# Two-branch layer on one core: all query tiles normalized inside the feed-forward, and the attention output of the last two heads moved into spare rows by DMA

## The chip, the cores and the metric

The kernel runs on one core of one Trainium2 chip. A core has a matrix engine (TensorE; PE in the profile, with its weight loads as PEld), a vector engine (VectorE; DVE), a scalar engine (ScalarE; ACT), a general engine (GpSimd; POOL) and a queue engine (SyncE; SP) that issues most of the transfers. Each engine takes its own instructions in order and waits for the others by semaphores. The metric is the time of the program on the device in microseconds (us); less is better.

## The reference

`x` has S = 2048 rows and D = 640 columns. Both branches read the layer norm of `x`; the result is `x + s * g`:

```python
xn = _layernorm(x, axis=-1)
# branch A: linear attention, H = 32 heads of Dh = 20
q, k, v = split(xn @ wqkv)
phi_q = concat([softmax(q @ w_phi), softmax(-(q @ w_phi))])     # 40 features a head; phi_k alike
kv = einsum("bhsf,bhsd->bhfd", phi_k, v);  z = einsum("bhsf->bhf", phi_k)
num = einsum("bhqf,bhfd->bhqd", phi_q, kv)
den = einsum("bhqf,bhf->bhq", phi_q, z)[..., None] + 1e-6
s = (num / den) @ wo
# branch B: feed-forward with F = 1536
g = silu(gelu(xn @ w1 + b1) @ w2 + b2)
return x + s * g
```

## The kernel before, in words

Precision: float32 operands are split into a high and a low part (hi, lo), and a product is three matmuls (hi with hi, and the two mixed ones), summed in PSUM. So most products are counted in threes (PASSES).

**Early stage** (to about 256 us): layer norm, projections to K, V and Q, the exponentials of the features, the state kv and z. The exponentials of the queries, not yet normalized, go to `e_dram`, sixteen tiles of 128 rows.

**Feed-forward** (256 to about 570 us): 12 units (halves of the rows times 6 groups of F columns; `units`), each about 25.8 us of TensorE: 54 "up" matmuls (L616), the activations (ScalarE L621 and its high copy L623, the low part on VectorE L627), then 60 "down" matmuls (L645) in two halves, `down(..., 0)` and `down(..., 1)`. The order on each engine is as the code is written out (manual schedule); nothing reorders it.

Into the units the **query normalization** is placed, tile by tile (`q_norm`): the tile is loaded from `e_dram` (L685), GpSimd multiplies it by z (L691), VectorE makes two reductions (L340) and some small operations, GpSimd scales the tile (L345), and SP stores it to `phi_dram` (L708). The table `QN` says which unit carries which tiles: units 1 to 5 one each, 7 to 9 two each, 10 one, 6 and 11 none. Tiles 4 to 7 are left to the last stage (`late_q`).

Weights are loaded raw (L144), split by ScalarE (L136, L400), GpSimd or VectorE (L138, L401). After unit 5 the half of the rows changes; the gate results of the first half of the units (`y0` to `y4`, called `held`) go through Silu in unit 6 and are stored to `g_dram` in unit 7 (L858). Buffers of 128 x 1280 or 128 x 1024 floats (`slab`) are shared in turn by eq, ez, hs, y and phi tiles: who gets a slab waits for its last user, the y store among them.

**Last stage** (from about 556 us): four chunks of 512 rows, in the order (2, 3, 0, 1). For each chunk `num_groups` transposes the normalized tiles (L735, copy L738), multiplies them with a block-diagonal form of kv (`bdk`, L746, for 30 heads in five groups j = 0 to 4; `bdl`, L753, for the last two heads, j = 5), and splits the outputs into `oT` tiles (hi on ScalarE L749, lo on VectorE L750). An `oT` tile holds six heads as 2 x 64 columns, of which 60 each are used. The last two heads have a tile of their own, `oTl`, with three copies of their 40 rows (120 rows: hi, hi and lo), selected by `lowsel` and `midsel`. Then `finish` makes the output blocks of 128 columns, five a chunk: 15 matmuls `oT` by `wo` and one `oTl` by `wol` (L804), which does the three passes at once; VectorE multiplies by the gate (L809), GpSimd adds x (L810; VectorE for the last blocks) and SP stores (L814). Gates of chunks 2 and 3 are loaded from `g_dram` (L788); those of chunks 0 and 1 come straight from the feed-forward through Silu on ScalarE (L796). x is loaded two blocks ahead (L784). The transposes and products of the next chunk are made between the blocks of the one before; those of the first chunk stand inside `down(..., 1)` of the last unit.

Transfers on SP are issued in the order of the code. SP's and ScalarE's transfers share eight semaphores in turn, so each one waits for the eighth before it.

Of the kernel before, what the change touches and what calls it, by code (L numbers as in the profile page):

```python
# [45 lines left out]
def hedgehog_gated_mlp_kernel(ctx: ExitStack, tc: tile.TileContext, x, xt_in, wqk, bd, wv, wo, w1, b1, w2, b2, out_t):  # L46
# [62 lines left out]
    for h in range(3):  # L109
# [4 lines left out]
    lowsel = const.tile([P, 1], F32, name="lowsel")  # L114
    nc.gpsimd.memset(lowsel[:], -1.0)
    nc.gpsimd.affine_select(out=lowsel[:], in_=lowsel[:], pattern=[[0, 1]],
                            compare_op=OP.is_ge, fill=0.0, base=-80, channel_multiplier=1)
    midsel = const.tile([P, 1], F32, name="midsel")
    nc.gpsimd.memset(midsel[:], -1.0)
    nc.gpsimd.affine_select(out=midsel[:], in_=midsel[:], pattern=[[0, 1]],  # L120
                            compare_op=OP.is_ge, fill=0.0, base=-40, channel_multiplier=1)
    nc.gpsimd.affine_select(out=midsel[:], in_=midsel[:], pattern=[[0, 1]],
                            compare_op=OP.is_ge, fill=0.0, base=79, channel_multiplier=-1)
    const.tile([P, 8], F32, name="align")
    bdk = const.tile([P, 10, 64], F32, name="bdk")
    bdl = const.tile([P, 120], F32, name="bdl")
# [436 lines left out]
    def kv_rest():  # L563
        kv_acc(NT - 1, phis.pop(NT - 1), vs.pop(NT - 1))
        kvr = const.tile([P, 360], F32, name="kvr")
        nc.gpsimd.memset(kvr[64:96, 320:360], 0.0)
        nc.gpsimd.memset(kvr[96:, 240:360], 0.0)
        for p, a, b in ((P, 0, 240), (96, 240, 320), (64, 320, 360)):
            nc.scalar.activation(kvr[:p, a:b], kvp[0][:p, a:b], AF.Copy)
        return kvr  # L570


    def kv_state(kvr):
        nc.gpsimd.memset(bdk[:, :, 60:], 0.0)
# [4 lines left out]
        nc.vector.tensor_tensor(bdk[:120, :, :60].rearrange("p f (h d) -> p f h d", d=20),  # L579
                                s3[:, :, None, :20].to_broadcast([120, 10, 3, 20]),  # L580
                                mask[:120, None, :, None].to_broadcast([120, 10, 3, 20]), op=OP.mult)
        for r in range(3):
            nc.vector.tensor_tensor(bdl[:80, 40 * r:40 * r + 40].rearrange("p (h d) -> p h d", d=20),
                                    ps[:80, None, 320:340].to_broadcast([80, 2, 20]),
                                    mask[:80, :2, None].to_broadcast([80, 2, 20]), op=OP.mult)
# [95 lines left out]

    def q_load(t):
        e = slab(F32, "eq")
        ef = e[:].rearrange("p a b -> p (a b)")
        nc.sync.dma_start(ef, e_dram[t])  # L685
        return ef

    def q_norm(t, ef):
        ez = slab(F32, "ez")
        zv = ez[:].rearrange("p a b -> p (a b)")  # L690
        nc.gpsimd.tensor_tensor(zv, ef, zf, op=OP.mult)  # L691
# [12 lines left out]
        nc.vector.tensor_tensor(r3, r3, den[:, :, None].to_broadcast([P, 32, 2]), op=OP.mult)  # L704
        yield
        scale_heads(ef, rc)
        yield
        nc.sync.dma_start(phi_dram[t], ef)  # L708

    def load_wol():  # L710
        raw = row([P, D], F32, "raw")
        for r in range(3):
            nc.sync.dma_start(raw[40 * r:40 * r + 40, :], wo[640:680, :])
        wol_h = row([P, D], F32R, "wolh")
        wol = row([P, D], F32R, "wol")
        nc.vector.tensor_copy(wol_h[:120, :], raw[:120, :])
        nc.vector.scalar_tensor_tensor(wol[:120, :], wol_h[:120, :].bitcast(F32), midsel[:120, :], raw[:120, :],
                                       op0=OP.mult, op1=OP.add)
        return wol


    def load_phi(c):
        tl = [slab(F32R, "phi", (P, 2 * D)) for _ in range(TPC)]
        for i in range(TPC):
            nc.sync.dma_start(tl[i][:].bitcast(F32), phi_dram[TPC * c + i])
        return tl
# [14 lines left out]
    def num_m(j, oT, p, n, ph):  # L741
# [9 lines left out]
        else:  # L751
            for a, b in ((0, 64), (64, 120)):
                nc.tensor.matmul(po[a:b, :256], bdl[:n, a:b], ph[:n, :256], start=True, stop=True)  # L753
            o2 = oT[1]
            nc.scalar.activation(o2[:120, 0, sl], po[:120, :256], AF.Copy)
            nc.vector.scalar_tensor_tensor(o2[:120, 1, sl], o2[:120, 0, sl].bitcast(F32), lowsel[:120, :],
                                           po[:120, :256], op0=OP.mult, op1=OP.add)

    def num_groups(phi, oT, size=4):
        steps = [(j, p) for p in range(2) for j in range(6)]  # L760
        before = []
        for k in range(0, 12, size):
            now = [(j, p, *num_t(phi, p, j)) for j, p in steps[k:k + size]]
            for j, p, n, ph in before:
                num_m(j, oT, p, n, ph)
            before = now
            yield
        for j, p, n, ph in before:
            num_m(j, oT, p, n, ph)
        yield  # L770
# [6 lines left out]
    ORDER = (2, 3, 0, 1)  # L777

    def load_res(i):
        if i < NCH * KC:  # L780
            c, d = divmod(i, KC)
            c = ORDER[c]
# [7 lines left out]
    def gate(i):  # L790
        if i < NCH * KC:
            c, d = divmod(i, KC)
            c = ORDER[c]
            if c < 2:
                y = ys[d][:, c, :]
                nc.scalar.activation(y, y, AF.Silu, bias=b2t[:, d:d + 1])  # L796
                gates[c, d] = y

    def finish(c, d, oT, last):
        ps = bankB()  # L800
        steps = [(wo_s[j][:, b, d * P:(d + 1) * P], oT[0][j][:, a, :]) for j in range(5) for a, b in PASSES]
        steps.append((wol[:120, d * P:(d + 1) * P], oT[1][:120, 1, :]))
        for n, (w, o) in enumerate(steps):
            nc.tensor.matmul(ps[:], w, o, start=n == 0, stop=n == 15)  # L804
        xr, gt = xres.pop((c, d)), gates.pop((c, d))
        for o in range(2):
            sl = slice(o * W2, (o + 1) * W2)
# [3 lines left out]
            if last:  # L811
                nc.sync.dma_start(out_t[d * P:(d + 1) * P, c * CW + o * W2:c * CW + (o + 1) * W2], xr[:, sl])
        if not last:
            nc.sync.dma_start(out_t[d * P:(d + 1) * P, c * CW:(c + 1) * CW], xr[:])  # L814
# [3 lines left out]
    QN = {1: (8,), 2: (9,), 3: (10,), 4: (11,), 5: (12,), 7: (13, 14), 8: (15, 0), 9: (1, 2), 10: (3,)}  # L818
    units = NH * NG

    def w2_raw(g):
        return [load_raw(w2[f * P:(f + 1) * P, :]) for f in range(g * GF, (g + 1) * GF)]

# [9 lines left out]
    for unit in range(units):  # L833
# [14 lines left out]
        else:  # L848
            wo_r = [load_raw(wo[j * P:(j + 1) * P, :]) for j in range(5)]
            phi = load_phi(ORDER[0])  # L850
# [55 lines left out]
        if not more:  # L906
# [4 lines left out]
            wo_s = [split_w(r[:], "wo", "pool", late) for j, r in enumerate(wo_r)]  # L911
# [4 lines left out]
        dn = down(g, w2g, hs, 0)  # L916
# [6 lines left out]
        next(dn)  # L923
        next(w1f, None)
# [12 lines left out]
        if not more:  # L937
            break
# [14 lines left out]
    wol = load_wol()  # L953
    oT = new_oT(late)
    qe[4] = q_load(4)
    load_res(0)
    load_res(1)
    for _ in down(g, w2g, hs, 1, num_groups(phi, oT, 3)):
        pass
# [3 lines left out]
    def late_q():  # L963
        qn = q_norm(4, qe.pop(4))
        next(qn)
        for t in range(4, 8):
            if t < 7:
                qe[t + 1] = q_load(t + 1)
            next(qn)
            yield  # L970
            next(qn)
            yield
            next(qn)
            next(qn)
            yield
            next(qn, None)
            if t < 7:
                qn = q_norm(t + 1, qe.pop(t + 1))
                next(qn)
            yield  # L980

    lq = late_q()
    for ci, c in enumerate(ORDER):
        nxt = iter(())
# [3 lines left out]
        for d in range(KC):  # L988
            load_res(ci * KC + d + 2)
            finish(c, d, oT, ci == NCH - 1 and d >= 3)  # L990
            next(lq, None)
            gate(ci * KC + d + 2)
            if ci == 0 and d % 2 == 0:
                next(lq, None)
            next(nxt, None)
            if ci + 2 < NCH and d == (0 if ci == 0 else 3):
                phin = load_phi(ORDER[ci + 2])
            next(lq, None)
        if ci + 1 < NCH:
            oT = oTn  # L1000
# [3 lines left out]
def _layout(A_x, A_wqkv, A_w_phi, A_wo, B_w1, B_b1, B_w2, B_b2):  # L1004
# [5 lines left out]
    wo = np.zeros((680, D), a["wo"].dtype)  # L1010
    for k in range(10):
        wo[64 * k:64 * k + 60] = a["wo"][60 * k:60 * k + 60]
    wo[640:] = a["wo"][600:]
# [37 lines left out]
```

## Time and profile before

| | |
|---|---|
| median of 3 runs | 686.83 us (685.87 to 687.21) |
| profiled execution | 688.63 us |
| its span in the trace | 686.9 us (1.7 us of the execution lie outside) |
| granted TensorE clock | 0.999 |
| HBM read and written | 79.85 and 45.10 MB, 182 GB/s over the span |

The span is cut into 40 slices in the page; a digit is the busy share in tenths:

```profile
PE   8899999999999999999999999999999999999997
DVE  4788566886876456677978774676977655774232
POOL 1355244859577355866968853636456640783221
```

A slice is 17.2 us. TensorE's line has nines from the third slice to the last but one: a high digit says that the engine has instructions nearly all the time, and only the chain of waits says whether the end hangs on them. VectorE and GpSimd vary by stage, and where both are near nine (around slice 25 and 31) the units carry two query tiles. Rows of other views are shown below where they are used. A row of the groups reads: line, engine, operation, tiles, shapes, count, then total busy time and mean of one. Where a matmul of the program shows as two records, the count of records is said.

### The profile page before, as it was taken

What the parts mean: (1) busy time and instruction counts of PE and PEld (TensorE: products, weight loads), DVE (VectorE), ACT (ScalarE), POOL (GpSimd) and SP (SyncE); (2) the same over time, 40 slices, a digit from 0 to 9 for tenths busy, and PEclk for the clock granted to TensorE, in tenths of its full rate; (3) what the DMA queues carried; (4) which work ended last, traced back from release to release, by engine and by line L of the source; (5) the groups of instructions that cost most, each with busy time, mean ns of one, the idle gap of its engine ahead of it and who ended that gap; (6) DMA issues with size and microseconds to landing.
All of it is one profiled execution on the core that took longest, in us unless ns stands there. A gap on an engine that the chain in (4) does not pass through costs nothing.

```text
span 686.9 us, 11941 instructions
## 1 busy us (share of the span) xinstructions
PE 676.7 (99%) x4713; PEld 590.6 (86%) x4713; DVE 455.5 (66%) x730; ACT 251.3 (37%) x398; POOL 375.6 (55%) x336
## 2 busy tenths in 40 slices
PE   8899999999999999999999999999999999999997
PEld 8899999999999998888887888888888887777875
DVE  4788566886876456677978774676977655774232
ACT  3332313323332237244353347633233354425430
POOL 1355244859577355866968853636456640783221
PEclk9999999999999999999999999999999999999999
DMA  9820052734261153329687697376364491886623
GB/s 339 305 88 2 3 150 81 242 79 149 51 216 59 80 171 134 115 70 329 211 301 260 210 421 319 90 266 240 140 206 153 145 396 49 314 295 210 231 93 107
DMA packets 73966, 125.73 MB, mean 183 GB/s; under 512 B 5694, under 2 KB 42558, under 8 KB 73014
## 3 DMA queue, kind: packets, MB, share of 16 engines
q1 hardware_dynamic: 71606, 114.48, 48.9%
q10 hardware_dynamic: 2304, 10.49, 4.2%
q8 instruction: 37, 0.61, 0.4%
q14 instruction: 19, 0.16, 0.1%
HBM read 79.85 MB, written 45.10 MB: 182 GB/s over the span
## 4 chain that ended last, share of the span: by engine, by line
PE 90%; DVE 5%; ACT 1%; issue 1%; DMA 1%; POOL 1%; SPq 0%; DVEq 0%; POOLq 0%; ACTq 0%
PE pA L306 30%; PE pB L645 22%; PE pB L616 18%; PE pB L804 11%; PE pB L746 3%; PE pB L735 2%; PE kv L377 2%; PE pA L163 2%; DVE y L654 2%; DVE xhi L670 1%; DMA xt<-in_x_dram 1%; PE pA L292 1%; PE pB L753 1%; DVE rc L340 0%; PE pB L590 0%
## 5 line engine op out<-in xcount | busy, mean ns | idle before, releaser
L645 PE MATMUL pB<-hs,w2s 128*128 128x512 f32 x720 | 167.1, 390 | 0.0
L645 PEld LDWEIGHTS pB<-hs,w2s 128*128 128x128 f32 x720 | 134.7, 188 | 29.2 <-PE pB L746 0.8
L616 PE MATMUL pB<-xp,w1s 128*128 128x512 f32 x324 | 81.4, 390 | 1.0 <-DVE pB L888 1.0
L616 PE MATMUL pB<-xd,w1s 128*128 128x512 f32 x324 | 79.3, 389 | 0.0
L332 ACT ACTIVATE e<-e 128x1280 f32<-128x1280 f32 x32 | 40.7, 1272 | 91.5 <-POOL e L327 91.0
L804 PE MATMUL pB<-oT,wo 128*128 128x512 f32 x300 | 72.9, 394 | 0.0
L616 PEld LDWEIGHTS pB<-xp,w1s 128*128 128x128 f32 x324 | 60.7, 188 | 13.9 <-DVE pB L888 1.4
L654 DVE TENSOR_TENSOR y<-pB,y 128x512 f32<-128x512 f32 x100 | 63.9, 680 | 12.3 <-PE pB L645 12.1
L616 PEld LDWEIGHTS pB<-xd,w1s 128*128 128x128 f32 x324 | 60.8, 188 | 12.6
L804 PEld LDWEIGHTS pB<-oT,wo 128*128 128x128 f32 x300 | 55.4, 188 | 14.8 <-ACT ph L738 1.2
L345 POOL TENSOR_TENSOR e<-e,rc 128x1280 f32<-128x1280 f32 x16 | 39.0, 2440 | 48.5 <-DVE rc L365 48.2
L345 POOL TENSOR_TENSOR eq<-eq,rc 128x1280 f32<-128x1280 f32 x16 | 38.0, 2372 | 50.0 <-DVE rc L704 50.0
L327 POOL TENSOR_TENSOR e<-nr,e 128x640 f32<-128x640 f32 x32 | 45.4, 1421 | 33.5 <-DVE nr L326 30.7
L306 PE MATMUL pA<-wv,xp 128*128 128x320 f32 x384 | 61.0, 312 | 0.8 <-DVE nr L326 0.4
L621 ACT ACTIVATE pB<-pB,b1t 128x512 f32<-128x512 f32 x48 | 31.8, 662 | 77.3 <-DVE pB L888 28.4
L306 PE MATMUL pA<-wk,xp 128*128 128x320 f32 x384 | 59.9, 311 | 0.0
L306 PE MATMUL pA<-wq,xp 128*128 128x320 f32 x384 | 59.0, 309 | 0.0
L306 PEld LDWEIGHTS pA<-wv,xp 128*128 128x128 f32 x384 | 56.9, 188 | 1.7 <-issue 0.7
L306 PEld LDWEIGHTS pA<-wq,xp 128*128 128x128 f32 x384 | 56.9, 188 | 0.1
L306 PEld LDWEIGHTS pA<-wk,xp 128*128 128x128 f32 x384 | 56.8, 188 | 0.1
L691 POOL TENSOR_TENSOR ez<-eq,zrep 128x1280 f32<-128x1280 f32 x16 | 47.3, 2953 | 1.1 <-PE pB L753 1.1
L401 POOL TENSOR_TENSOR w1s<-raw,w1s 128x640 fp32r<-128x640 f32 (+1 forms) x18 | 25.7, 1429 | 36.8 <-ACT w1s L400 29.6
(139 smaller groups left out, 1046.0 us busy)
## 6 DMA issues: line engine op xcount, KB each, us to landing
raw<-in_w_dram SPq DMA_DIRECT2D x42, 320.0 KB, 4.4
e_dram<-e ACTq DMA_DIRECT2D x16, 640.0 KB, 3.3
eq<-e_dram SPq DMA_DIRECT2D x16, 640.0 KB, 6.9
phi_dram<-eq SPq DMA_DIRECT2D x16, 640.0 KB, 3.4
phi<-phi_dram SPq DMA_DIRECT2D x16, 640.0 KB, 9.5
xt<-in_x_dram SPq DMA_DIRECT2D x16, 320.0 KB, 4.8
xres<-in_xt_dram SPq DMA_DIRECT2D x20, 256.0 KB, 4.5
out_dram<-xres SPq DMA_DIRECT2D x18, 256.0 KB, 3.0
```

The costliest lines, as they stand in the source:

```text
L306: nc.tensor.matmul(ps[:, hf, :HALF], stat_x(q, o, k, a), ws[k][:, b, hf * HALF:(hf + 1) * HALF], start=n == 0, stop=n == 3 * KC - 1)
L327: nc.gpsimd.tensor_tensor(e5[:, :, :, 1, :], nr[:, :, :, None].to_broadcast([P, 2, 16, DH]), e5[:, :, :, 0, :], op=OP.subtract)
L332: nc.scalar.activation(ef, ef, AF.Exp)
L345: nc.gpsimd.tensor_tensor(e3, e3, rc[:, :, None].to_broadcast([P, 64, DH]), op=OP.mult)
L401: nc.gpsimd.tensor_tensor(sl[:, 1, :n], src, sl[:, 0, :n].bitcast(F32), op=OP.subtract)
L616: nc.tensor.matmul(bank[ch][:], tl[:, a, off + wo_:off + wo_ + P], mov(blk, b), start=new and n == 0, stop=n == len(mms) - 1, skip_group_c ...
L621: nc.scalar.activation(ps, ps, AF.Gelu_apprx_tanh, bias=b1t[:, f:f + 1])
L645: nc.tensor.matmul(ps[:], ws[i][:, b, d * P:(d + 1) * P], hs[o][i][:, a, :], start=i == n == 0, stop=(i, n) == (GF - 1, 2), skip_group_che ...
L654: nc.vector.tensor_tensor(y, ps[:], y, op=OP.add)
L691: nc.gpsimd.tensor_tensor(zv, ef, zf, op=OP.mult)
L746: nc.tensor.matmul(po[64 * e:64 * e + 64, :256], bdk[:n, 2 * j + e, :], ph[:n, e * 256:(e + 1) * 256], start=True, stop=True)
L804: nc.tensor.matmul(ps[:], w, o, start=n == 0, stop=n == 15)
```

## The change

1. **Last two heads.** `wol`, `load_wol`, `lowsel` and `midsel` go. The columns of `bdk` are laid out anew: of each 16, 15 hold three heads' parts and every sixteenth is empty, and the rows of `wo` are laid out likewise, with the last two heads' 40 rows in the sixteenth places. `bdl` makes 40 columns with one matmul. The result, hi and lo, goes to `oTl` (40 rows), and `spread` moves 8 rows of it (32 KB) into rows 15, 31, 47, ... of each of the five `oT` tiles, by a DMA on ScalarE's queue, five a chunk. A block has 15 matmuls.
2. **Query tiles.** `QN` places all 16 in the units 1 to 11: one in each of 1 to 6, two in each of 7 to 11. `late_q` goes.
3. **Order.** Chunks run 0, 1, 2, 3, and groups in the order j = 5, 0, 1, 2, 3, 4. In the last unit, the splits of `wo` and the first chunk's products (sizes 2, 3, 3, 2, 2) start in the last call of `down(..., 0)`.
4. **Small moves.** In the last stage, output stores are issued one block later (`put`, `put_old`), and phi tiles are loaded one by one.

The core of the diff:

```diff
-    bdl = const.tile([P, 120], F32, name="bdl")
+    bdl = const.tile([P, 40], F32, name="bdl")
...
-    def load_wol():
...
-            for a, b in ((0, 64), (64, 120)):
-                nc.tensor.matmul(po[a:b, :256], bdl[:n, a:b], ph[:n, :256], start=True, stop=True)
+            nc.tensor.matmul(po[:40, :256], bdl[:n, :], ph[:n, :256], start=True, stop=True)
...
+    def spread(j, oT):
+        nc.scalar.dma_start(oT[0][j][15::16].bitcast(F32), oT[1][8 * j:8 * j + 8].bitcast(F32))
...
+    def num_groups(phi, oT, sizes=(4, 4, 4)):
+        steps = [(j, p) for j in (5, 0, 1, 2, 3, 4) for p in range(2)]
+        before, whole = [], []
+        def products(group):
+            for j, p, n, ph in group:
+                num_m(j, oT, p, n, ph)
+                if p and j < 5:
+                    whole.append(j)
+        def spreads():
+            while whole:
+                spread(whole.pop(0), oT)
+        for size in sizes:
+            now = [(j, p, *num_t(phi, p, j)) for j, p in steps[:size]]
+            del steps[:size]
+            spreads()
+            products(before)
+            before = now
+            yield
+        spreads()
+        products(before)
+        spreads()
         yield
...
-    ORDER = (2, 3, 0, 1)
+    ORDER = (0, 1, 2, 3)
...
-        steps.append((wol[:120, d * P:(d + 1) * P], oT[1][:120, 1, :]))
         for n, (w, o) in enumerate(steps):
-            nc.tensor.matmul(ps[:], w, o, start=n == 0, stop=n == 15)
+            nc.tensor.matmul(ps[:], w, o, start=n == 0, stop=n == 14)
...
-    QN = {1: (8,), 2: (9,), 3: (10,), 4: (11,), 5: (12,), 7: (13, 14), 8: (15, 0), 9: (1, 2), 10: (3,)}
+    QN = {1: (0,), 2: (1,), 3: (2,), 4: (3,), 5: (4,), 6: (5,), 7: (6, 7), 8: (8, 9), 9: (10, 11), 10: (12, 13), 11: (14, 15)}
...
+        dn = down(g, w2g, hs, 0, None if more else delayed(groups, 4))
```

Three places show how the instructions stand. The first is SP's queue at units 6 and 7 (raw is a weight row, eq a query tile, phi_dram its normalized form, y a stored gate; "x2" is two in a row). Before:

```order
L660 DMA xp<-xp_dram 128x2048
L708 DMA phi_dram<-eq 128x1280
L144 DMA raw<-in_w_dram 128x640 x4
L685 DMA eq<-e_dram 128x1280 x2
L144 DMA raw<-in_w_dram 128x640 x2
L685 DMA eq<-e_dram 128x1280 x2
L858 DMA g_dram<-y_3244 128x1024
L858 DMA g_dram<-y_3250 128x1024
```

And of the change:

```order
L651 DMA xp<-xp_dram 128x2048
L679 DMA phi_dram<-eq 128x1280
L134 DMA raw<-in_w_dram 128x640 x4
L688 DMA eq<-e_dram 128x1280 x2
L679 DMA phi_dram<-eq 128x1280
L134 DMA raw<-in_w_dram 128x640 x2
L688 DMA eq<-e_dram 128x1280 x2
L879 DMA g_dram<-y_3237 128x1024
L879 DMA g_dram<-y_3243 128x1024
```

A second phi_dram store (tile 5, which unit 6 now normalizes) stands ahead of two raw loads, two eq loads and the y stores.

The second is ScalarE in unit 7: the activations (L621, now L612) and the high copies into hs (L623, now L614), with what each waits for; a DMAHW semaphore is that of a transfer, here of a g_dram store that frees the slab. Before:

```order
L623 ACTIVATE hs<-pB 128x512 [waits DMAHW6_49,Activation_49]
L621 ACTIVATE pB<-pB,b1t 128x512 [waits DVE_49]
L623 ACTIVATE hs<-pB 128x512 [waits DMAHW7_49,Activation_49]
L621 ACTIVATE pB<-pB,b1t 128x512 [waits DVE_49]
L623 ACTIVATE hs<-pB 128x512 [waits PE_49,Activation_49]
```

And of the change:

```order
L614 ACTIVATE hs<-pB 128x512 [waits PE_49,Activation_49,Pool_49]
L612 ACTIVATE pB<-pB,b1t 128x512 [waits DVE_49]
L614 ACTIVATE hs<-pB 128x512 [waits PE_49,Activation_49,Pool_49]
L612 ACTIVATE pB<-pB,b1t 128x512 [waits DVE_49]
L614 ACTIVATE hs<-pB 128x512 [waits DMAHW0_49,Activation_49]
```

The wait for the first y store has moved from the first high copy of the unit to the third.

The third is TensorE at the start of the last stage (ph is the copy of the transposed tile; a bdk or bdl matmul of the program shows as two records in the trace). Before:

```order
L746 MATMUL pB<-ph,bdk 64x256 x4
L753 MATMUL pB<-ph,bdl 64x256
L753 MATMUL pB<-ph,bdl 56x256
L645 MATMUL pB<-hs,w2s 128x512 x6
L804 MATMUL pB<-oT,wo 128x512 x15
L804 MATMUL pB<-oTl,wol 128x512
L735 MATMUL pB<-identr,phi 120x128 x16
```

And of the change:

```order
L739 MATMUL pB<-ph,bdk 64x256 x4
L636 MATMUL pB<-hs,w2s 128x512 x6
L808 MATMUL pB<-oT,wo 128x512 x15
L728 MATMUL pB<-identr,phi 80x128 x4
L728 MATMUL pB<-identr,phi 120x128 x8
L808 MATMUL pB<-oT,wo 128x512 x15
L728 MATMUL pB<-identr,phi 120x128 x16
```

The last products ahead of the first block are now those of the fifth group of bdk instead of bdl's, then six down matmuls, and the block has 15 matmuls, the last three of which read the fifth oT tile.

More of the change, by code (lines that the diff above doesn't have):

```diff
@@ L113, in hedgehog_gated_mlp_kernel @@
                                 compare_op=OP.is_ge, fill=0.0, base=40 * h + 39, channel_multiplier=-1)
[L114 to L124, printed above, removed]
+    const.tile([P, 24], F32, name="align")
     bdk = const.tile([P, 10, 64], F32, name="bdk")
-    bdl = const.tile([P, 120], F32, name="bdl")
+    bdl = const.tile([P, 40], F32, name="bdl")
     def load_x(t):
@@ L564, in kv_rest @@
         kv_acc(NT - 1, phis.pop(NT - 1), vs.pop(NT - 1))
-        kvr = const.tile([P, 360], F32, name="kvr")
+        kvr = const.tile([P, 376], F32, name="kvr")
         nc.gpsimd.memset(kvr[64:96, 320:360], 0.0)
@@ L573, in kv_state @@
     def kv_state(kvr):
-        nc.gpsimd.memset(bdk[:, :, 60:], 0.0)
+        nc.gpsimd.memset(bdk[:, :, 15::16], 0.0)
         ps = bankB()
@@ L578, in kv_state @@
         s3 = ps[:120, :320].rearrange("p (f r) -> p f r", r=32)
[L579 to L585, printed above, removed]
+        for h in range(3):
+            nc.vector.tensor_scalar(
+                bdk[:120].rearrange("p f (q c) -> p f q c", c=16)[:, :, :, 5 * h:5 * h + 5],
+                s3[:, :, :20].rearrange("p f (q i) -> p f q i", i=5), mask[:120, h:h + 1], None, op0=OP.mult)
+        nc.vector.tensor_tensor(bdl[:80].rearrange("p (h d) -> p h d", d=20),
+                                ps[:80, None, 320:340].to_broadcast([80, 2, 20]),
+                                mask[:80, :2, None].to_broadcast([80, 2, 20]), op=OP.mult)
     def kv_norm(kvr):
@@ L679, in x_forms, with put, put_old @@
         nc.sync.dma_start(xd_dram[:, :, 1, at(p)], tt)
+    stores, late_store = [], [False]
+    def put(dst, src):
+        if late_store[0]:
+            stores.append((dst, src))
+        else:
+            nc.sync.dma_start(dst, src)
+    def put_old(n):
+        for _ in range(n):
+            nc.sync.dma_start(*stores.pop(0))
     def q_load(t):
@@ L707, in q_norm, with load_phi_tile @@
         yield
-        nc.sync.dma_start(phi_dram[t], ef)
-    def load_wol():
[L711 to L719, printed above, removed]
-    def load_phi(c):
[L723 to L726, printed above, removed]
+        put(phi_dram[t], ef)
+    def load_phi(c):
+        return [load_phi_tile(c, i) for i in range(TPC)]
+    def load_phi_tile(c, i):
+        t = slab(F32R, "phi", (P, 2 * D))
+        nc.sync.dma_start(t[:].bitcast(F32), phi_dram[TPC * c + i])
+        return t
     def num_t(phi, p, j):
@@ L822, in w2_raw, with last_mid, delayed @@
         return [load_raw(w2[f * P:(f + 1) * P, :]) for f in range(g * GF, (g + 1) * GF)]
+    wo_s = []
+    def last_mid():
+        for k, _ in enumerate(num_groups(phi, oT, (2, 3, 3, 2, 2))):
+            for _ in range((2, 2, 1, 0, 0, 0)[k]):
+                wo_s.append(split_w(wo_r[len(wo_s)][:], "wo", "pool", late))
+            for _ in range((0, 1, 1, 1, 1, 1)[k]):
+                next(q1, None)
+            for _ in range((0, 0, 1, 0, 0, 0)[k]):
+                next(q2, None)
+            yield
+    def delayed(mid, n):
+        for _ in range(n):
+            yield
+        yield from mid
     kvr = kv_rest()
@@ L915, in hedgehog_gated_mlp_kernel @@
         next(w1f, None)
-        dn = down(g, w2g, hs, 0)
+        if not more:
+            oT = new_oT(late)
+            groups = last_mid()
+        dn = down(g, w2g, hs, 0, None if more else delayed(groups, 4))
         next(dn)
@@ L923, in hedgehog_gated_mlp_kernel @@
         next(dn)
+        if not more:
+            next(dn)
+            next(dn)
+            break
         next(w1f, None)
@@ L952, in hedgehog_gated_mlp_kernel @@
             ys[:] = [None] * KC
-    wol = load_wol()
-    oT = new_oT(late)
-    qe[4] = q_load(4)
+    hs = (None, (h12, h22))
     load_res(0)
     load_res(1)
-    for _ in down(g, w2g, hs, 1, num_groups(phi, oT, 3)):
+    for _ in down(g, w2g, hs, 1, groups):
+        pass
+    for _ in q2:
         pass
@@ L961, in hedgehog_gated_mlp_kernel @@
     gate(1)
[L963 to L982, printed above, removed]
+    late_store[0] = True
     for ci, c in enumerate(ORDER):
-        nxt = iter(())
+        nxt, phi2 = iter(()), []
         if ci + 1 < NCH:
@@ L988, in hedgehog_gated_mlp_kernel @@
         for d in range(KC):
+            old = len(stores)
             load_res(ci * KC + d + 2)
             finish(c, d, oT, ci == NCH - 1 and d >= 3)
-            next(lq, None)
             gate(ci * KC + d + 2)
-            if ci == 0 and d % 2 == 0:
-                next(lq, None)
             next(nxt, None)
-            if ci + 2 < NCH and d == (0 if ci == 0 else 3):
-                phin = load_phi(ORDER[ci + 2])
-            next(lq, None)
+            put_old(old if ci + 1 < NCH else len(stores))
+            if ci + 2 < NCH and d >= ci:
+                while len(phi2) < min(TPC, 2 * (d + 1)):
+                    phi2.append(load_phi_tile(ORDER[ci + 2], len(phi2)))
         if ci + 1 < NCH:
-            oT = oTn
+            oT, phin = oTn, phi2
     ffn.close()
@@ L1009, in _layout @@
     bd = np.zeros((P, 6, 120), a["wphi"].dtype)
[L1010 to L1013, printed above, removed]
+    wo = np.zeros((D, D), a["wo"].dtype)
+    w4 = wo.reshape(10, 4, 16, D)
+    w4[:, :, :15] = a["wo"][:600].reshape(10, 3, 4, 5, D).transpose(0, 2, 1, 3, 4).reshape(10, 4, 15, D)
+    w4[:, :, 15] = a["wo"][600:].reshape(10, 4, D)
     for h in range(H):
```

28 lines of the change are left out of this document (7 added, 21 removed).

## The prediction, made before the changed kernel ran

> **What bounds the kernel now.** I read the page's totals first, then its slices, the chain, and last the waits of TensorE.
>
> ```profile
> PE 676.7 (99%) x4713; PEld 590.6 (86%) x4713; DVE 455.5 (66%) x730; ACT 251.3 (37%) x398; POOL 375.6 (55%) x336
> PEclk9999999999999999999999999999999999999999
> PE 90%; DVE 5%; ACT 1%; issue 1%; DMA 1%; POOL 1%; SPq 0%; DVEq 0%; POOLq 0%; ACTq 0%
> PE pA L292 <- DVE xt L197: 1.4, 2, 1.3
> PE pB L616 <- DVE pB L888: 1.0, 1, 1.0
> ...
> PE pA L306 <- POOL wv L138: 0.2, 1, 0.2
> ```
>
> TensorE is busy for 676.7 of the span's 686.9 us at full granted clock, and 90% of the chain is its matmuls. Its waits list six groups, 5.2 us in all (shown: the largest, the only one inside the feed-forward, and the least). So a matmul taken away shortens the run by its full length, work on other engines counts only if it ends later than TensorE needs it, and there is hardly any idle time to win back. The sum below stands on matmuls removed and on waits that may come new.
>
> **What is removed.** Rows of the groups by shape, then pieces of the chain in the last stage (start, length, piece):
>
> ```profile
> L804 PE MATMUL pB<-oTl,wol 120*128 120x512 f32 x20 | 7.9, 395 | 0.0
> L753 PE MATMUL pB<-ph,bdl 80*64 80x256 f32 x16 | 4.8, 379 | 0.0
> L753 PE MATMUL pB<-ph,bdl 80*56 80x256 f32 x16 | 4.8, 379 | 0.0
> 579.68 3.63 PE pB L804 x16
> 591.27 3.86 PE pB L804 x16
> 603.36 0.43 PE pB L753 x4
> ```
>
> The 395 ns of one is the time in the pipeline, with neighbours overlapped; what one matmul costs is its share of a piece. An uninterrupted output block of 16 takes 3.63 us, 0.227 each. All 20 wol matmuls go: 20 x 0.227 = **4.5 us**. A last-heads product is now two program matmuls (64 and 56 columns), four records, 0.43 us; one 40-column matmul leaves two records, 0.215 us. Eight such products: 8 x 0.215 = **1.7 us**. Against it, the last unit's down matmuls are interrupted once more; a block broken into took 3.86 instead of 3.63, so +0.2. TensorE's work: -4.5 - 1.7 + 0.2 = **-6.0 us**. Transposes, block-diagonal products and 15 matmuls a block stay as many; bdk's empty columns cost nothing, since the matmul still has 64.
>
> **What is moved into the units.** One query tile more stands in units 6 and 10, two in 11. Windows of units 6, 8, 10 and 11 (PE, PEld, DVE, ACT, POOL, then clock, DMA share, GB/s), and the steps of a tile:
>
> ```profile
> 414.10:440.30 26.20, 26.20 (x119) 21.67 (x118) 13.56 (x23) 20.36 (x25) 8.88 (x9) 1.00 0.44 178
> 466.20:492.00 25.80, 25.80 (x115) 21.36 (x114) 20.18 (x34) 7.07 (x11) 13.62 (x6) 1.00 0.57 209
> 517.80:543.70 25.90, 25.90 (x116) 21.46 (x115) 19.59 (x32) 8.98 (x15) 20.56 (x15) 1.00 0.26 95
> 543.70:569.50 25.80, 25.80 (x146) 20.91 (x147) 13.87 (x20) 13.79 (x26) 9.02 (x6) 1.00 0.93 352
> L691 POOL TENSOR_TENSOR ez<-eq,zrep 128x1280 f32<-128x1280 f32 x16 | 47.3, 2953 | 1.1 <-PE pB L753 1.1
> L345 POOL TENSOR_TENSOR eq<-eq,rc 128x1280 f32<-128x1280 f32 x16 | 38.0, 2372 | 50.0 <-DVE rc L704 50.0
> L340 DVE TENSOR_REDUCE rc<-eq 128x64 f32<-128x1280 f32 x16 | 23.6, 1476 | 3.5 <-DMA eq<-e_dram 3.5
> ```
>
> A tile is 2.95 + 2.37 = 5.3 us of POOL and two reductions of 1.48 with small operations, about 4.5 us, of DVE. Unit 6 rises to 18.1 DVE and 14.2 POOL of 26.2; unit 11 to 22.9 and 19.7 of 25.8. Unit 8 carries two tiles with 20.18 us of DVE and TensorE busy throughout. Unit 10 is the tight one: POOL 20.56 + 5.3 = 25.9 of 25.9. I cost it at nothing, since unit 11 reads what POOL makes last there only in its down half, 13 us into the unit; without that cover its overrun, one scaling of 2.4 us at most, would show. The last stage gives up the four late tiles. The loads and DVE work for wol lay beside matmuls, so their removal wins nothing.
>
> **The new wait: unit 7.** Unit 6 had no tile. Now SP's queue there holds a phi_dram store that must wait for POOL's scaling of tile 5, and the five g_dram stores are behind it. Timeline rows (start, busy), chain pieces, and windows of the stretch:
>
> ```profile
> 439.44 1.02 POOL L401 TENSOR_TENSOR w1s<-raw,w1s 128x384 fp32r<-128x384 f32 x1
> 439.68 1.04 SPq L685 DMA_DIRECT2D eq<-e_dram  x2
> 440.77 3.27 SPq L858 DMA_DIRECT2D g_dram<-y  x5
> 412.62 2.00 SPq L144 DMA_DIRECT2D raw<-in_w_dram  x4
> 448.99 0.60 ACT L623 ACTIVATE hs<-pB 128x512 fp32r<-128x512 f32 x1 [3.20 <-DMA g_dram<-y]
> 451.99 0.60 ACT L623 ACTIVATE hs<-pB 128x512 fp32r<-128x512 f32 x1
> 452.69 0.69 DVE L627 TENSOR_TENSOR hs<-pB,hs 128x512 fp32r<-128x512 f32 x1 [0.24 <-ACT hs L623]
> 440.33 12.24 PE pB L616 x54
> 452.57 13.60 PE pB L645 x60
> 445.80:452.00 6.20, 6.20 (x29) 5.11 (x28) 2.82 (x5) 2.42 (x5) 3.61 (x2) 1.00 1.02 417
> ```
>
> Before, the first y store is issued at 440.77 and its landing, 8.2 us later, frees the buffer of unit 7's first hs at 448.99; TensorE doesn't feel it, its down half starts at 452.57. After, the scaling follows POOL's w1 split (439.44 + 1.02 = 440.46, + 2.37 = 442.83); then SP issues the phi store (0.3), two raw loads (2.00/4 each) and two eq loads (1.04): the y store goes at about 445.3. The buffer it frees now goes to the third hs copy. That one's low part is read by the tenth down matmul or so, at 452.57 + 9 x 0.227 + some delay = 455.0; less 0.60 for the high copy and 0.69 for the low one, y0 must land by 453.7. With the old 8.2 us it lands at 453.5 and costs nothing; if the 1,280 KB now ahead of it (phi store, two raws) delay it by their time at 417 GB/s, 3.1 us more, at 456.6, and TensorE waits 2.9. Between 0 and 2.9 I take **+1.5**: in this stretch the DMA engines are full (1.02), but 4.5 us later than before they have also drained part of what was ahead. Queued behind the waiting hs copy on ScalarE is only the same unit's next activation.
>
> **What is added: 20 spreads.** Each is 32 KB on ScalarE's queue, 5 a chunk. Nothing like it is in the trace; nearest rows (KB each, us to landing), and the last products of chunk one (chain piece, then hi and lo copies):
>
> ```profile
> st_dram<-pst SPq DMA_DIRECT2D x4, 2.0 KB, 3.0
> out_dram<-xres SPq DMA_DIRECT2D x4, 128.0 KB, 1.9
> gt<-g_dram SPq DMA_DIRECT2D x10, 256.0 KB, 5.8
> 147.12 0.33 ACTq L359 DMA_DIRECT2D e_dram<-e  x1
> 576.65 1.01 PE pB L746 x8
> 577.70 0.86 DVE L750 TENSOR_TENSOR oT<-pB,oT 128x256 fp32r<-128x256 f32 x2 [0.32 <-ACT oT L749]
> 578.10 1.58 PE pB L645 x6
> ```
>
> Between 1.9 and 5.8 us from issue to landing; I take 2.5, nearest to the two small transfers in a stretch where the queues are not full. Place of the tightest, chunk 0's last: products start at T, their low parts are done at T + 1.9 (577.70 + 0.86 against 576.65), the spread is issued about T + 2.0; its rows are read by the 13th matmul of the first block, at T + 1.01 + 1.58 + 12 x 0.227 = T + 5.3. So 3.3 us are hidden. In the other chunks a whole block (3.4) stands between: about 4.5 us are hidden. At 2.5 us the cost is nothing. Twenty issues of 0.33 on ScalarE lie in its idle time.
>
> The Trainium skill, page "DMA: Bandwidth & Descriptors", section "Rules for kernel authors", speaks against such transfers: under 64 KB one pays mostly overhead, so they should be merged; its section "Anatomy of one DMA — SWDGE (gpsimd) path" gives some 2.0 us fixed plus the bytes at 436 GB/s. That makes an estimate of 2.1 us for a spread, which the 1.9 to 3.0 us of the rows bear out; paid in the open, the twenty would be +42 us in place of 0, but the slack just worked out covers each.
>
> Chunk 0's phi tiles are loaded once the last stores of unit 10 are issued, and four rather than two are needed, at about 561.
>
> ```profile
> 543.23 1.57 POOL L138 TENSOR_TENSOR w2s<-raw,w2s 128x640 fp32r<-128x640 f32 x1
> 545.16 7.07 SPq L725 DMA_DIRECT2D phi<-phi_dram  x8
> phi<-phi_dram SPq DMA_DIRECT2D x8, 640.0 KB, 10.8
> ```
>
> Tile 13's scaling comes behind the w2 split at 543.23 (+ 1.57 + 2.37 = 547.2) and its store 0.3 later; issued at 547.5, at the 10.8 us of these rows the phi loads land by 558 to 559: 2 to 3 us spare, cost taken as 0, else up to the lateness of one tile, 1.6 us (640 KB at 417 GB/s).
>
> **Sum.** Against the profiled execution's 688.63 us (span 686.9 and 1.7 around it): -6.0 + 1.5 = -4.5, 684.1. That execution is 1.8 above the median of 686.83; on the median, **682.3 us**.
>
> **Rivals.**
> - *The unit 7 wait stays hidden* (y0 by 453.7): -6.0, 680.8. For it: the same store needed only 8.2 us in a full stretch.
> - *More waits of the unit 7 kind*: a phi tile late, or a unit whose DVE falls behind, as L888's wait of 1.0 shows; 1.5 to 3 us beyond the forecast, 683.8 to 687.
> - *Spreads land late; slower.* If each takes what gt takes, 5.8 us (32 KB in lines on 8 partitions, behind 256 KB loads), chunk 0 loses 5.8 - 3.3 = 2.5 and three chunks 5.8 - 4.5 = 1.3 each: +6.4, so -6.0 + 1.5 + 6.4 = +1.9, 688.7. From (L - 3.3) + 3(L - 4.5) = 4.5, it decides from a landing time L of 5.3 us. Against it: the small-transfer rows.
> - *Less than counted*: the switches between products and blocks get cheaper too; below 680.2.
>
> **How the numbers follow.** Forecast with a stall of 0.3 to 2.9 (681.1 to 683.7): 0.50. Hidden, 680.2 to 681.1: 0.24. More waits, up to 687: 0.16, three quarters of it under 685.4. Slower: 0.05. Below 680.2: 0.05. The range 680.0 to 685.2 leaves out some 0.15. About 0.2%, 1.4 us, is what a measurement here tells from no change: faster (below 685.4) 0.50 + 0.24 + 0.12 + 0.05 - 0.03 for misjudged bounds = 0.88; same 0.07; slower 0.05.
>
> **What would show it.** Right: no L804 row with wol, 15 to a block at about 3.4 us; bdl pieces of 0.21; TensorE's busy time near 670.7; one new wait of TensorE in unit 7, on the low hs of DVE, behind a ScalarE copy released by g_dram<-y; spreads landing in 2 to 3 us. Wrong: that wait absent (then 680.8); waits of L808 for oT spreads; waits in units 10 and 11 on POOL's splits; idle TensorE before the first transposes of chunk 0.

## The result, and the profile after

| | before | after |
|---|---|---|
| median | 686.41 us (685.87 to 687.21, 4 runs) | 682.07 us (681.47 to 682.85, 4 runs) |
| ratio after to before | | 0.9934, 95% interval 0.9920 to 0.9948 |
| profiled execution, span | 688.63, 686.9 us | 682.85, 681.1 us |

The change makes the kernel 0.66% faster, 4.3 us; 682.3 was predicted. The page of the changed kernel begins:

```profile
PE 672.5 (99%) x4677; PEld 586.3 (86%) x4677; DVE 452.9 (66%) x728; ACT 251.5 (37%) x398; POOL 376.6 (55%) x331
```

Of its waits of TensorE (engine, line, what was waited for: us in all, times, longest) one is behind unit 0:

```profile
PE pB L636 <- ACT hs L614: 0.2, 1, 0.2
```

TensorE still bounds it. Busy time fell by 4.2 us, not by the 6.0 forecast, while the span fell by 5.8: so the two traces differ in more than the matmuls taken away. Where, is read by cutting the span at the first up matmul of each unit (timeline, start and length):

```profile
254.74 1.55 PE L607 MATMUL pB<-xp,w1s 128*128 128x512 f32 x6
360.38 1.52 PE L607 MATMUL pB<-xp,w1s 128*128 128x512 f32 x6
386.46 1.52 PE L607 MATMUL pB<-xp,w1s 128*128 128x512 f32 x6
438.51 1.52 PE L607 MATMUL pB<-xp,w1s 128*128 128x512 f32 x6
465.16 1.52 PE L607 MATMUL pB<-xp,w1s 128*128 128x512 f32 x6
542.68 1.52 PE L607 MATMUL pB<-xp,w1s 128*128 128x512 f32 x6
```

These are units 0, 4, 5, 7, 8 and 11. The same rows of the kernel before:

```profile
255.41 1.55 PE L616 MATMUL pB<-xp,w1s 128*128 128x512 f32 x6
360.98 1.52 PE L616 MATMUL pB<-xp,w1s 128*128 128x512 f32 x6
388.12 1.52 PE L616 MATMUL pB<-xp,w1s 128*128 128x512 f32 x6
440.17 1.52 PE L616 MATMUL pB<-xp,w1s 128*128 128x512 f32 x6
466.01 1.52 PE L616 MATMUL pB<-xp,w1s 128*128 128x512 f32 x6
543.53 1.52 PE L616 MATMUL pB<-xp,w1s 128*128 128x512 f32 x6
```

Before unit 7 the changed kernel is already 1.66 us ahead (0.67 at unit 0, and 1.0 in unit 4, which took 388.12 - 360.98 = 27.14 before and takes 386.46 - 360.38 = 26.08 now). Unit 7 takes 465.16 - 438.51 = 26.65 instead of 466.01 - 440.17 = 25.84: **0.81 lost**. From unit 11's start to the last matmul it is 133.89 (676.57 - 542.68) instead of 138.60 (682.13 - 543.53): **4.71 won**; the tail behind the last matmul gives the remaining 0.2.

The last matmuls in the chain of the changed kernel, and the pieces that the prediction named (start, length, piece):

```profile
563.15 0.99 PE pB L745 x4
...
579.17 3.42 PE pB L808 x15
...
588.24 0.77 PE pB L745 x3
...
589.07 0.16 PE pB L745
...
655.93 20.64 PE pB L808 x90
```

The last piece of before reads:

```profile
659.99 22.14 PE pB L804 x96
```

Six blocks take 1.50 us less, 0.25 each. But the two bdl products of a chunk take 0.77 + 0.16 = 0.93 (0.99 in the first chunk), where before two positions of 0.43 made 0.86: half the bdl matmuls are gone and nothing is won. Why can be read from stretches of 0.12 us at the start of such a product, bdl records only (PE and its weight loads, number of records in brackets, then clock, DMA share, GB/s). First the kernel before, then the changed one:

```profile
603.18:603.30 0.12, 0.11 (x2) 0.10 (x2) 1.00 0.70 273
588.16:588.28 0.12, 0.11 (x1) 0.11 (x2) 1.00 1.23 239
```

Before, two records lie side by side in it, one of 64 columns and one of 56; now there is one. Adding the pieces of the last stage by line, in us:

| work | before | after | measured | forecast |
|---|---|---|---|---|
| output blocks | 75.17 | 70.34 | -4.83 | -4.5 |
| bdl products | 3.44 | 3.78 | +0.34 | -1.7 |
| bdk products | 19.28 | 18.98 | -0.30 | 0 |
| transposes | 13.69 | 13.57 | -0.12 | 0 |
| down matmuls of unit 11 | 14.57 | 14.85 | +0.28 | +0.2 |
| sum | | | -4.6 | -6.0 |

The wait in unit 7, in the timeline and the chain of the changed kernel:

```profile
438.76 2.36 POOL L335 TENSOR_TENSOR eq<-eq,rc 128x1280 f32<-128x1280 f32 x1
441.15 0.32 SPq L679 DMA_DIRECT2D phi_dram<-eq  x1
...
450.75 2.20 PE L636 MATMUL pB<-hs,w2s 128*128 128x512 f32 x9
...
452.54 0.60 ACT L614 ACTIVATE hs<-pB 128x512 fp32r<-128x512 f32 x1 [2.25 <-DMA g_dram<-y]
453.18 0.69 DVE L618 TENSOR_TENSOR hs<-pB,hs 128x512 fp32r<-128x512 f32 x1 [2.38 <-ACT hs L614]
453.19 0.30 PEld L636 LDWEIGHTS pB<-hs,w2s 128*128 128x128 f32 x2 [0.67 <-ACT hs L614]
453.92 10.98 PEld L636 LDWEIGHTS pB<-hs,w2s 128*128 128x128 f32 x49 [0.43 <-DVE hs L618]
```

```profile
444.01 8.45 DMA g_dram<-y
```

It is the predicted one: SP's phi_dram store waits for GpSimd's scaling of tile 5 (438.76 + 2.36), the first y store is issued behind it, lands 8.45 us later, at 452.46, and lets the third high copy go. When that copy is done, at 453.14, nine down matmuls are over (450.75 + 2.20 = 452.95), and the tenth has waited. The list of waits shows 0.2 of it, counted from the end of the ninth's record; at 0.227 us each the tenth would have started at 452.79, so it is 0.4 late. A second wait, of the twelfth for the low part, stands in the row of the weight loads (0.43) and not in that of the matmuls. The length of the unit shows it all.

### The profile page after: what moved, and what is told of

The parts are those of the page before. It is cut to its first block, busy times and chain, and to the rows that moved or that the text cites. A ratio compares the mean times of both kernels' runs of the same rounds, so it can differ in the third digit from the quotient of the medians.

```text
span 681.1 us, 11880 instructions
## 1 busy us (share of the span) xinstructions
PE 672.5 (99%) x4677; PEld 586.3 (86%) x4677; DVE 452.9 (66%) x728; ACT 251.5 (37%) x398; POOL 376.6 (55%) x331
## 4 chain that ended last, share of the span: by engine, by line
PE 87%; DMA 5%; issue 3%; POOL 2%; DVE 1%; SPq 1%; ACT 0%; POOLq 0%; ACTq 0%
PE pA L296 30%; PE pB L636 20%; PE pB L607 17%; PE pB L808 10%; PE pB L739 3%; PE pB L728 2%; PE pA L153 2%; DMA xp<-xp_dram 2%; PE kv L367 2%; DMA raw<-in_w_dram 1%; DMA g_dram<-y 1%; POOL w1s L391 1%; DMA folds<-in_wqk_dram 1%; PE pA L282 1%; PE pB L745 1%
## 5 line engine op out<-in xcount | busy, mean ns | idle before, releaser
L612 ACT ACTIVATE pB<-pB,b1t 128x512 f32<-128x512 f32 x48 | 31.8, 662 | 75.9 <-DVE pB L909 27.1
```

Of the source, the lines that this page charges most:

```text
L612: nc.scalar.activation(ps, ps, AF.Gelu_apprx_tanh, bias=b1t[:, f:f + 1])
```

## The experiments

They ran at different times and not all on one chip; the kernel before, run beside each group, had medians of 686.24 to 687.01 us. So medians of different experiments compare to some tenths only, and the lengths of stages in the traces carry the argument.

**The kernel before, profiled once more** (no edit).

> The kernel before, profiled once more, to see which differences between the two traces belong to the change. In the first pair TensorE starts unit 0 0.67 us earlier after the change (255.41 against 254.74) and unit 5 another 1.0 us earlier (a wait of 1.0 for L888 in unit 4). Theory, both are luck of one execution: this profile shows the fold wait near 0.5 us, or no wait at L888, and a span of about 685 us. Rival, both belong to the kernel: the waits are 1.0 and 1.0 again and the span is 686.9 within 0.3.

687.34 us in its one run, span 685.6. Its first matmuls of units 0, 4 and 5:

```profile
254.40 1.55 PE L616 MATMUL pB<-xp,w1s 128*128 128x512 f32 x6
360.02 1.52 PE L616 MATMUL pB<-xp,w1s 128*128 128x512 f32 x6
386.14 1.52 PE L616 MATMUL pB<-xp,w1s 128*128 128x512 f32 x6
```

Unit 0 starts even earlier than in the changed kernel, and unit 4 takes 26.12. So the 1.66 us ahead of unit 7 belong to the executions, not to the change. This trace has two short waits in the last stage instead (0.4 for phi, 0.3 for oT), and 139.3 there. By it the last stage's gain would be 5.4 us and not 4.7. No trace of the changed kernel or of its variants lists these waits; whether the change removes them for good, two traces of the kernel before don't show, and the prediction has no term for them.

**A second bdl matmul, in other columns.**

```diff
             nc.tensor.matmul(po[:40, :256], bdl[:n, :], ph[:n, :256], start=True, stop=True)
+            nc.tensor.matmul(po[64:104, :256], bdl[:n, :], ph[:n, :256], start=True, stop=True)
```

> The changed kernel with a second bdl matmul beside each of the eight (columns 64 to 104 of the same bank, result not used). Theory: matmuls of 64 columns or fewer in the lower and the upper half of the array run side by side, so the change's removal of one of two saved nothing; a chunk's bdl pieces stay at 0.93 us, time as after the change (682.1, within 0.3). Rival, as predicted: each matmul costs 0.215 us, pieces of 1.4 to 1.9 us a chunk and +1.7 us in all (683.8).

681.75 us (681.26 to 682.17, 4 runs), the last stage 133.96. In its chain L745 is the first matmul's line and L746 the added one's:

```profile
561.50 0.34 PE pB L745
561.84 0.01 PE pB L746
561.85 0.21 PE pB L745
562.05 0.01 PE pB L746
```

Each record of the added matmul ends 0.01 us behind its partner: they run side by side, and eight more matmuls cost 0.07 us.

**The same matmul twice, in the same columns.**

```diff
             nc.tensor.matmul(po[:40, :256], bdl[:n, :], ph[:n, :256], start=True, stop=True)
+            nc.tensor.matmul(po[:40, :256], bdl[:n, :], ph[:n, :256], start=True, stop=True)
```

> The changed kernel with each bdl matmul issued a second time into the same 40 columns (the result is the same). It parts what made the second matmul free when it went to columns 64 to 104. Theory: the two halves of the columns work at once, and in the same columns they can't; each repeat costs its full two records, 2 x 0.21 = 0.43 us, a chunk's bdl pieces grow from 0.93 to about 1.8 us and the time by 8 x 0.43 = 3.4, to 685.5. Rival: a second matmul on the same moving data is free wherever it goes, or hidden in the gaps at the change of shape; then the time stays at 682.1 within 0.5.

685.61 us (685.13 to 686.54, 10 runs), ratio to before 0.9987 (0.9978 to 0.9997): 3.5 us above the changed kernel. In its chain:

```profile
562.18 0.56 PE pB L745 x2
562.73 0.43 PE pB L746 x2
```

Now each program matmul takes its own 0.43 (the first 0.56, after other shapes), and the last stage is 137.37, 3.5 longer. It is the place in the columns that makes the second one free, not its moving data or a gap at the change of shape. Nor does it wait for the place in PSUM that the first one writes: a chunk's two products in the changed kernel go to different buffers, in the same columns, and take 0.93.

**The g_dram stores issued in unit 6.**

```diff
-        if unit == NG + 1:
-            for d, o in enumerate(held):
-                nc.sync.dma_start(g_dram[d], o[:])
...
         next(xg, None)
+        if unit == NG:
+            for d, o in enumerate(held):
+                nc.sync.dma_start(g_dram[d], o[:])
         next(q1, None)
```

> The changed kernel with the five g_dram stores issued in unit 6, ahead of the phi_dram store of tile 5 and of the loads behind it. Theory: unit 7 lost 0.8 us (26.65 from start to start against 25.84) to the high copy that waits for the first y store; here the copy doesn't wait for a store, unit 7 takes 25.84 us again, and the time falls by 0.8 to about 681.3. Rival: the slots only shift the wait (the phi_dram store, the raw loads or the eq loads now come late behind 2.5 MB of stores), unit 7 or 8 loses 0.5 to 1 us and the time stays at 682 or above.

681.89 us (681.52 to 682.01, 4 runs). In its timeline the stores go out 26 us earlier, the third high copy waits for nothing, and the down matmuls run through:

```profile
417.76 15.51 SPq L961 DMA_DIRECT2D g_dram<-y  x5
...
450.20 0.60 ACT L614 ACTIVATE hs<-pB 128x512 fp32r<-128x512 f32 x1
...
450.62 3.56 PE L636 MATMUL pB<-hs,w2s 128*128 128x512 f32 x15
```

Unit 7 takes 25.84 again. The loss in it is shown to come from the late store; that the time falls by 0.8 is not: the median is 0.2 lower, less than the runs scatter.

**Without the spreads.**

```diff
-        nc.scalar.dma_start(oT[0][j][15::16].bitcast(F32), oT[1][8 * j:8 * j + 8].bitcast(F32))
+        pass
```

> The changed kernel without the 20 spreads (the last two heads are left out of the output). Theory: the spreads land inside their slack, so the time stays at 682.1 within 0.3 and the last stage (start of unit 11 to the last matmul) at 133.7. Rival: they cost something, by their issue on ScalarE's queue (0.57 us each) or by late landing; then the last stage shortens by 0.5 us or more.

681.73 us (681.42 to 683.16, 4 runs). Its last piece of the chain:

```profile
656.16 20.64 PE pB L808 x90
```

With unit 11 starting at 542.91 the last stage is 133.89, to the hundredth that of the changed kernel. The 20 transfers cost nothing where they stand.

**The last spread of each chunk twice.**

```diff
-        nc.scalar.dma_start(oT[0][j][15::16].bitcast(F32), oT[1][8 * j:8 * j + 8].bitcast(F32))
+        for _ in range(2 if j == 4 else 1):
+            nc.scalar.dma_start(oT[0][j][15::16].bitcast(F32), oT[1][8 * j:8 * j + 8].bitcast(F32))
```

> The changed kernel with each chunk's last spread issued twice; the second writes the same rows and so waits for the landing of the first, and the distance of the two issues is the landing time L of one spread. Theory: L is 2 to 3 us. In chunk 0 the rows are then there at 578.5 + 2L (first issue in the profile of the changed kernel) and read by the 13th matmul of the block that starts at 579.2, at 581.9: a wait of 0.6 to 2.6 us; the other chunks have about 4.5 us and wait 0 to 1.5. In all +0.6 to +4. Rival (the slower case of the prediction): L is over 4 us, the wait over 4.5 us in chunk 0 alone and the time above 688.

685.45 us (684.18 to 686.22, 10 runs), 3.4 above the changed kernel. The chain of the first chunk:

```profile
577.27 2.21 DMA oT<-oTl
...
579.51 2.22 DMA oT<-oTl
...
581.87 0.94 PE pB L809 x3
```

In this chunk one spread lands 2.2 us after its issue (2.5 was taken). The 13th matmul waits 1.2 us for the second one, and only for that: a single one, landed at 579.49, would have been there 1.2 us ahead of the 12 matmuls' end at 580.7. TensorE's list of waits has 2.0 us of this kind, in three chunks:

```profile
PE pB L809 <- DMA oT<-oTl: 2.0, 3, 1.2
```

The last stage is 136.79, 2.9 longer: as in unit 7, the list holds a part of the loss. Later in the stage a spread takes longer, as a piece of the third chunk shows:

```profile
630.41 3.65 DMA oT<-oTl
```

The semaphore records of the changed kernel's own trace say the same: 2.2 to 2.3 us in the first chunk, 2.3 to 4.6 in the others. The last spread of a later chunk has 5.3 us (issued at 630.1, read at 635.4 in the changed kernel) and lands after 3.9 at most.

The Trainium skill, page "DMA: Bandwidth & Descriptors", section "Anatomy of one DMA — SWDGE (gpsimd) path", gives for transfers issued from GpSimd about 2.0 us and the bytes at 436 GB/s, an estimate of 2.1 us for 32 KB. Here, from ScalarE's queue, it was 2.2 in the first chunk, near that, and up to 4.6 in the later ones, which it doesn't cover; either costs nothing as long as matmuls cover it.

**A 16th matmul back in each block.**

```diff
+        steps.append((wo_s[4][:120, 0, d * P:(d + 1) * P], oT[0][4][:120, 0, :]))
         for n, (w, o) in enumerate(steps):
-            nc.tensor.matmul(ps[:], w, o, start=n == 0, stop=n == 14)
+            nc.tensor.matmul(ps[:], w, o, start=n == 0, stop=n == 15)
```

> The changed kernel with a 16th matmul of 120 rows back in each of the 20 output blocks (it repeats one product of the fifth group, so the output is off by that). Theory: each costs its share of a block, 0.23 to 0.25 us, in all +4.6 to +4.9; a block of 16 takes 3.63 again, the last stage (133.9 from the start of unit 11 to the last matmul) grows to 138.6 and the time to 686.8. Rival: part of the change's gain comes from the reordering of the last stage and not from these matmuls; then this gives back clearly less, under 3.5 us.

687.02 us (686.40 to 687.51, 10 runs), ratio to before 1.0009 (1.0000 to 1.0019): 4.95 above the changed kernel. In its chain:

```profile
658.60 22.16 PE pB L809 x96
```

The last stage is 138.77, 4.88 longer, where the change had won 4.71: these 20 matmuls account for the whole gain.

**The two bdl products side by side.**

```diff
...
+            o = 64 * p
+            if p == 0:
+                last_heads[:] = [bankB()]
+            po = last_heads[0]
-            nc.tensor.matmul(po[:40, :256], bdl[:n, :], ph[:n, :256], start=True, stop=True)
+            nc.tensor.matmul(po[o:o + 40, :256], bdl[:n, :], ph[:n, :256], start=True, stop=True)
+            if p == 0:
+                return
...
+            for p in range(2):
+                sl, o = slice(256 * p, 256 * p + 256), 64 * p
+                nc.scalar.activation(o2[:40, 0, sl], po[o:o + 40, :256], AF.Copy)
+                nc.vector.tensor_tensor(o2[:40, 1, sl], po[o:o + 40, :256], o2[:40, 0, sl].bitcast(F32), op=OP.subtract)
```

> The changed kernel with the two bdl products of a chunk in the lower and the upper half of the array's columns (rows 0 and 64 of one bank), so that they run side by side; the copies bring both to the same 40 rows. Theory: two records' time instead of four, a chunk's bdl pieces fall from 0.93 to about 0.5 us, the last stage from 133.9 to 132.2 and the time from 682.0 to 680.3. Rival: copies across rows or the shared bank hold TensorE up by as much, and the last stage stays at 133.5 or above.

680.44 us (680.01 to 681.05, 4 runs), ratio to before 0.9916 (0.9901 to 0.9931), last stage 132.54. In its chain the four records of a chunk:

```profile
561.96 0.56 PE pB L751 x4
```

0.56 in place of 0.99. Four chunks make about 2.2 us, where the kernel before had 3.44: 1.2 of the 1.7 us that the prediction had booked under bdl, and it takes pairing the matmuls to get them.

**Both edits.**

> Both together: bdl products side by side, and the g_dram stores issued in unit 6. Theory: the two add, last stage 132.2 and unit 7 at 25.84 us, time 679.5 to 680.2. Rival: as for each alone; then 681.5 or above.

680.06 us (679.92 to 681.53, 4 runs), ratio 0.9917 (0.9900 to 0.9933); unit 7 at 25.84 and the last stage at 132.56.

**Three kernels beside one another on one chip**, five rounds: the changed one, the one with early stores, and the one with both edits.

> The changed kernel again, beside the next two on one chip, so that they can be compared with it and not only with the kernel before. Theory: 681.7 to 682.1 us, unit 7 between 0.1 and 1.0 us longer than 25.84, the last stage 133.9. Rival, if the first pair of traces showed the change and not luck: unit 0 starts at 254.74 within 0.1 and unit 4 takes 26.08 within 0.1.

> The changed kernel with the g_dram stores in unit 6, again. Theory: unit 7 at 25.84 in the trace and the time 0.3 to 0.8 us below the changed kernel's of the same call (the mean of what unit 7 lost in seven traces is 0.5). Rival: the shorter unit 7 is given back elsewhere, and the two times agree within 0.15.

> Both edits (bdl products side by side, g_dram stores in unit 6), again. Theory: 1.35 us from the last stage and 0.3 to 0.8 from unit 7, so 1.6 to 2.2 us below the changed kernel of the same call. Rival: under 1.2 us.

| | median, us | ratio to before | unit 7 | last stage |
|---|---|---|---|---|
| changed | 682.66 (681.97 to 685.09, 5) | 0.9938 (0.9924 to 0.9952) | 26.25 | 133.89 |
| stores in unit 6 | 682.14 (681.24 to 682.92, 5) | 0.9936 (0.9922 to 0.9950) | 25.84 | 133.88 |
| both edits | 680.41 (680.15 to 680.73, 4) | 0.9907 (0.9893 to 0.9921) | 25.84 | 132.55 |

Both edits together run 2.2 us below the changed kernel, each of their runs below each of its: the best version here. The early stores alone differ by 0.5 us in the median while the runs overlap and the ratios agree; so their gain is seen in the trace of unit 7, not settled in the time. The changed kernel's unit 0 starts at 256.82 in this trace, 2.1 us later than in the first, and unit 4 takes 26.38; over the twelve traces of the changed kernel and its variants unit 0 starts between 253.7 and 256.8: the start of the program varies by more than the smaller terms of this study.

## Why the prediction came out right, and where it was wrong

- **The blocks** (-4.5): right; -4.83 by the pieces, 4.88 in the last stage when put back.
- **bdl** (-1.7): wrong, and it is the step that failed. "One 40-column matmul leaves two records, 0.215 us" took the 0.43 of four records as a sum. The 64- and 56-column matmuls had run side by side in two halves of the columns, so the pair took what one alone takes, 0.43; dropping one saved nothing, and the chunk's two products now stand alone at 0.93. The Trainium skill, page "TensorEngine Tiling (Array Packing)", section "Tiling Modes", states that with at most 64 columns there are two independent tiles that work in parallel; the trace agrees (0.01 us for the partner, 0.43 in the same columns). The sign was in the trace of before: of the four records in 0.43 us, two start within the same 0.12 us.
- **Unit 7** (+1.5, between 0 and 2.9): mechanism and place right, the size too large. Eight traces of kernels with the stores in unit 7 lost 0.10, 0.34, 0.39, 0.41, 0.42, 0.52, 0.81 and 1.01 us there, 0.5 in the mean; four with the stores in unit 6 lost 0.00. The store landed 8.45 us after its issue, near the old 8.2 and not the 9.9 that +1.5 stands for (453.7 + 1.5 - 445.3); that the queue had drained by then fits this and was not tested by itself. The deadline was off the other way: 453.7 is 13.5 us behind the unit's start, the store landed 13.95 behind it (452.46 - 438.51), and that cost 0.81 and not 0.4. The tenth matmul waits for the high copy already, not for the low part, and the twelfth waits once more.
- **Cover of the tiles moved** (0): right, with less to spare than was taken. Units 8 to 10 take 25.84 us, and no wait of TensorE is listed behind unit 7. GpSimd is at 21.5 us in unit 10, not 25.9 (a window of the changed kernel):

```profile
517.80:543.70 25.90, 25.90 (x116) 21.46 (x115) 20.34 (x30) 9.15 (x15) 21.50 (x14) 1.00 0.40 152
```

  Work of unit 10 runs over into unit 11 instead. GpSimd's weight splits for unit 11 in the kernel before, then in the changed kernel the scaling of unit 10's second tile and the splits behind it:

```profile
541.70 3.10 POOL L138 TENSOR_TENSOR w2s<-raw,w2s 128x640 fp32r<-128x640 f32 x2
545.81 2.37 POOL L335 TENSOR_TENSOR eq<-eq,rc 128x1280 f32<-128x1280 f32 x1 [4.95 <-DVE rc L707]
551.06 3.09 POOL L128 TENSOR_TENSOR w2s<-raw,w2s 128x640 fp32r<-128x640 f32 x2
```

  The splits end at 554.15, 0.9 us ahead of the down half that reads them (555.08); before, 11.1 us lay between (544.80 to 555.93). The prediction put the overrun at 2.4 us at most. Slices 25 and 31 of the kernel before, where VectorE and GpSimd were said to be both near nine, have the digits 4 and 3, and 7 and 6.
- **Spreads and phi loads** (0): right; in the tightest place, the first chunk, 2.2 us to landing where 3.4 are covered (issue at 578.5, read at 581.9 in the changed kernel), and the last stage is the same without them. The slower rival, which needed 5.3 us, falls, though spreads of later chunks took up to 4.6, more than the 2 to 3 that were named as the sign.
- **Sum**: -4.6 in the last stage + 0.5 in unit 7 = -4.1, measured -4.3; forecast -6.0 + 1.5 = -4.5. So 682.3 met 682.07 in part because two errors cancel: 1.4 us too much gain in the last stage (2.0 at bdl, less 0.6 won elsewhere in it) and 1.0 us too much loss in unit 7. What remains between the terms and the median, a few tenths, lies inside the scatter of the program's start. Against the second trace of before the last stage gains 5.4 and the sum is -4.9; which of the two is the usual one stays open.

## What to carry to other kernels

Where TensorE is busy throughout, price a matmul by what the chain loses without it: one that has a partner in the other half of the columns cost next to nothing to keep here and won nothing when it went, and one that stands alone can be paired. Compare two traces stage by stage, cut at the same instruction, and profile the old kernel twice, before a difference is put down to the change. A small transfer that moves rows between partitions, 2.2 to 4.6 us here, is free if enough matmuls stand between its issue and its reader; a store queued behind another engine's result is a wait for whoever needs its buffer.

## What was not expected of the hardware

Two matmuls of 40 columns on the same 80 rows, written to rows 0 and 64 of a bank, ended 0.01 us apart; in the same rows the second took 0.43 us. A wait of TensorE is partly hidden in the list of waits: unit 7 lost 0.81 us and 0.2 is listed; with each last spread issued twice the last stage lost 2.9 and 2.0 are listed.
